# Attention with a gated MLP on one core: where block sums, half additions and value loads stand in the unit order

## The chip, the core and the metric

The kernel runs on one core of a Trainium2 chip. Its five engines have queues of their own: TensorE (PE in the profile, its weight loads PEld) multiplies matrices, VectorE (DVE) and ScalarE (ACT) work on elements, GpSimd (POOL) does here half of an addition and issues a few transfers, and SyncE (SP) issues nearly all DMA transfers. An engine runs its instructions in the order of the program and waits on semaphores for the others. The metric is the device time of one execution in microseconds (us), as the median of several runs. One further execution is profiled; all rows are from that one.

## The reference

```python
xn = _layernorm(x, axis=-1)                       # x: 1 x 2048 x 512
q = (xn @ wq).reshape(B, Sq, H, Dh)               # H = 32 heads, Dh = 128
scores = einsum("bhqd,bhkd->bhqk", q, k_cache) * Dh ** -0.5     # 2048 keys
o = einsum("bhqk,bhkd->bhqd", softmax(scores), v_cache)
s = o.reshape(B, Sq, H * Dh) @ wo                 # 4096 -> 512
h  = gelu(layernorm(xn) @ w1);  hs = shifted(h) @ w2;  x1 = xn + hs
h2 = gelu(layernorm(x1) @ w3) @ w4
out = x + s * silu(x1 + h2)
```

The attention over 32 heads is nearly all of the work. The MLP's gate is computed first and stored in DRAM until the output is put together. Everything is in bf16 with sums in f32.

## The kernel before, in words

The main loop runs over 128 units. A unit is one head with one block of 512 queries; the order is 8 groups of 4 heads, in each group the 4 query blocks, in each block the 4 heads. So unit 16g + 4qt + hh is head hh of group g with query block qt. A unit has 8 slots (SPU), and the loop from L1131 on goes over all slots n = 8u + p and writes out by hand, for slot p of unit u, what each engine gets next. Every instruction is pinned to that order, so an operation that is entered in another slot stands at another place of its engine's queue.

In a slot, TensorE multiplies two key chunks of 128 with the unit's queries into one of two PSUM tiles (`s_slot`, `ps_s`), ScalarE exponentiates it (L446, `pT<-ps_s`), and TensorE multiplies the values with the exponentials of ten slots ago (`pv_slot`, `ps_o<-pT,vb`).

The denominators of the softmax come from VectorE: `add_first` (L452) adds the first two `pT` tiles of a unit in slot 4, the third tile is added in slot 6, the fourth in slot 0 of the next unit, then `fold` and `fold_last` shrink the result to 128x512. The third tile is added in one of two ways. Outside the set `APART` it is one VectorE addition of 128x2048 (`add_next`, L461). Inside, GpSimd adds one half in slot 6 and VectorE the other half in slot 0 of the next unit (`add_half`, both L457).

From there the sums take a way through SP's queue. In slot 3 of the next unit the folded tile is transposed by a DMA (`turn`, L494, `tT<-acc`); in slot 0 of the unit after that VectorE sums it (`turned_sums`, L499) and takes reciprocals (L505), SP writes them to DRAM (L507, `dr<-rc`), in slot 1 SP reads them back on all partitions (`bcast`, L511, `rb<-dr`), and in slot 7 VectorE scales the unit's output with them (`norm`, L523). SP issues in order, and a transfer that waits for a semaphore holds all behind it.

The query projections of pairs of heads (units 14 to 125) and most of the output projections are done with seven products in place of eight, on sums and differences of blocks. VectorE makes these:

- `x_sum(qt, i)` (L366): sums of blocks of the normalised input, four for each query block, sixteen in all, entered by the list at L1120. One of them is written in place into `xnT`.
- `w_sum(h, i)` (L375): differences of query weights for the pair of heads h, h+1, entered at L1123. For head pair 2 all four stand in unit 11.
- `wo_sum(g, i)` (L562): differences of the output weights of a group, entered at L1084, four for each group.
- `o_sum` (L571): sums of the attention outputs of a block.

TensorE's products (`ps_q`, `ps_wo`) follow in fixed slots. The `ps_wo` tile has one buffer, so the next product into it waits until VectorE has added the last one to the accumulators (`wo_take`, L596). The queries of a pair are put together by ScalarE and VectorE (L415, L423 to L431), the last piece (L431) in slot 6 of the unit ahead of the pair.

Loads for the next group are spread over the loop from L993: b is the first unit of a group's last query block. Keys come in four transposing transfers for each head (`load_k`, L147), values in two halves of 256 KB (`load_v`, L159), issued in slot 6 of units b-2, b-1 (first head), b+2, b+3, b+4, b+5, b+6 and b+7 (fourth head). At the end of each slot the entries of `todo` run, so a value load of slot 6 stands in SP's queue behind the turned sums of slot 3 and the key load of slot 5, and ahead of the reciprocals of the next unit. The last head's value tile has a column of ones and is loaded in four pieces; `open_vx` opens it and sets that column.

The pool for block sums (`pS`) opens only when the MLP's held products are done, in unit 7.

Of the kernel before, what the change touches and what calls it, by code (L numbers as in the profile page):

```python
# [11 lines left out]
BF16 = mybir.dt.bfloat16  # L12
# [5 lines left out]
def kernel(  # L18
# [16 lines left out]
    P = nc.NUM_PARTITIONS  # L35
# [3 lines left out]
    Sq, D = x2d.shape  # L39
# [11 lines left out]
    HG = 4  # L51
    NG = H // HG

    SPU = KC // 2
# [34 lines left out]
    qtp = ent(pool("qt", 6))  # L89
# [11 lines left out]
    pR = right.enter_context(pool("pR", side="right", reuse_waits="tile"))  # L101
# [21 lines left out]
    HEAD = 7  # L123
# [11 lines left out]
    def at(n, fn):  # L135
        todo[n].append(fn)
# [194 lines left out]
               xnT[:, dc, qt * 512:(qt + 1) * 512], dc == 0, dc == DC - 1)  # L331

    def q_copy(u, eng=None):
        pl, tag = (pR, "qR") if u < HEAD else (qtp, "qT")
        qT = pl.tile([P, 512], BF16, tag=tag, **(dict(bufs=HEAD) if u < HEAD else {}), name="qT")
        src, dst = st[u].pop("psq")[:], qT[:]
        if u in TURN:
            src = src.rearrange("d (r j) -> d j r", j=4)
            dst = dst.rearrange("d (j r) -> d j r", j=4)
        if eng is None:  # L340
            pin(nc.vector.tensor_copy(out=dst, in_=src))
        else:
            pin(nc.scalar.activation(out=dst, in_=src, func=ACT.Identity))
        st[u]["qT"] = qT[:]
# [208 lines left out]
    def wo_sum(g, i):  # L553
        w = wog[g]
        b11, b12, b21, b22 = (w[:, k, c] for k in (UP, DOWN) for c in (WL, WR))
        if i == 2 and g < NG - 2:
            out = b12
        else:
            j = 0 if i == 2 else i
            out = pS.tile([P, 2, D // 2], BF16, tag=f"tw{j}", bufs=TW[j], name="tw")[:]  # L560
        a, b = ((b12, b11), (b22, tw.get((g, 0))), (b22, b12), (b21, tw.get((g, 1))))[i]
        pin(nc.vector.tensor_tensor(out=out, in0=a, in1=b, op=ALU.subtract))  # L562
        tw[g, i] = out
# [426 lines left out]
    pS = None  # L990
    for h in range(HG):
        load_wo(h)
    for g in range(NG - 1):  # L993
        b = (g * QT + QT - 1) * HG
        for hh in range(HG):
            h = (g + 1) * HG + hh
            for i, u in enumerate(((-10, -9, -8, -7), (-6, -5, -2, -1) if g else (-4, -3, -2, -1), (1, 1, 2, 3), (4, 5, 5, 6))[hh]):
                at((b + u) * SPU + 5, lambda h=h, i=i: load_k(h, (i,)))
            for i in range(2):
                at((b + (-2, 2, 4, 6)[hh] + i) * SPU + 6, lambda h=h, i=i: load_v(h, (i,)))  # L1000
            if h == H - 1:
                at((b + 6) * SPU + 3, open_vx)
            at((b + (-3, -3, 0, 0)[hh]) * SPU + (5, 7)[hh % 2], lambda h=h: load_w(h))
            at((b - 4 - hh // 2) * SPU + (5, 7)[hh % 2], lambda h=h: load_wo(h))

# [47 lines left out]

    FIRST, LAST = 14, NU - 4
    BLOCK = [(g, qt) for g in range(NG - 1) for qt in range(QT)][1:-2]
    APART = range(2 * HG + 1, NU - 3)
    pairs = range(FIRST, LAST + 1, 2)
    q_plan = defaultdict(list)
    steps = defaultdict(list)
# [21 lines left out]
            which[u0 + n].append((o_sum, g, qt, i))  # L1081
    for g in range(NG - 1):
        u0 = ((g * QT + (g == 0)) * HG + 6) * SPU
        for i, n in ((0, -4), (2, -4 if 0 < g < NG - 2 else 4), (1, 4), (3, 12)):  # L1084
            o_early[u0 + n].append((wo_sum, g, i))
    for i, (qt, u) in enumerate((qt, qt * HG + 5 + j) for qt in range(1, QT) for j in range(2)):
        at(u * SPU + 6, lambda qt=qt, i=i: sa_clear(qt, i % 2))
# [29 lines left out]
        for fn, *args in plan.get(n, ()):  # L1117
            fn(*args)

    for j, u in enumerate((9, 9, 9, 9, 12, 12, 13, 13, 13, 16, 17, 17, 18, 19, 20, 20)):  # L1120
        at(u * SPU + 3, lambda qt=(j // 4 - 1) % QT, i=j % 4: x_sum(qt, i))
    for h in range(2, H, 2):
        for i, u in enumerate((((-4, -3, -3, -3), (-1, -1, 0, 0))[h % HG // 2] if h >= HG else (11,) * 4)):  # L1123
            o_early[(h // HG * QT * HG + u) * SPU + 4].append((w_sum, h, i))

    for v in range(1, NU):
# [242 lines left out]
```

## Time and profile before

| | us |
|---|---|
| median of three runs | 1224.51 |
| lowest and highest run | 1224.1 and 1224.75 |
| the profiled execution, its time | 1222.83 |
| the same, its span from first to last instruction | 1221.1 |
| granted TensorE clock, mean | 1.000 |

The page gives for each engine its busy time with the share of the span and the count of instructions, then the chain that ended last, followed back from the end, as shares by engine. A row of a stretch gives the window in us from the start of the span, its length, the busy time of PE, PEld, DVE, ACT and POOL with the count of instructions, the granted clock, the share of the DMA engines and their GB/s. A row in order of time gives start and duration in us, engine, line, operation, out<-in, the shape, the count of equal instructions merged into the row, and in brackets the idle time of the engine just before it with what ended it. Instructions on one engine overlap a little, so what one costs is the step from its start to the next start, which is shorter than its duration. Some matmul records are missing (a row then says x1 where others say x2), and ends of matmuls are modelled, so for TensorE too starts are compared. "DMA to landing" is the time from the issue of a transfer to its completion.

### The profile page before, as it was taken

The page shows a single profiled execution, that of the slowest core. Times are in us where ns is not written, and L with a number is a line of the kernel's source. Part 1 is how long each engine was busy: PE and PEld are TensorE (multiplying, and loading weights), DVE is VectorE, ACT ScalarE, POOL GpSimd, SP SyncE. Part 2 cuts the span into 40 slices and gives each one's busy share as a digit, 9 for nine tenths or more (in the row PEclk, how much of TensorE's full clock was granted, in tenths as well). Part 3 has the DMA queues.
Part 4 walks back from the last instruction along what each step waited for, and adds up shares of the span by engine and source line. Part 5 has one row for each costly group of instructions (what it writes and reads, how often), then busy time and mean ns, then how long its engine had stood idle before and what let it go on. Part 6 is the DMA issues. An engine that isn't in the chain of part 4 may idle for free.

```text
span 1221.1 us, 18821 instructions
## 1 busy us (share of the span) xinstructions
PE 1208.6 (99%) x6534; PEld 673.7 (55%) x6657; DVE 1089.9 (89%) x1931; ACT 1107.6 (91%) x1243; POOL 297.6 (24%) x221
## 2 busy tenths in 40 slices
PE   9999999999999999999999999999999999999998
PEld 6466444555555555555555555555555555555555
DVE  7863778999999999999999899999999999989997
ACT  6345999999999999999999999999999999999996
POOL 5300001233222222222222222222222222223320
PEclk9999999999999999999999999999999999999999
DMA  7662323434343434344344433444433534455552
GB/s 178 169 153 59 56 57 83 96 85 98 75 90 88 99 66 90 85 99 88 70 95 84 103 69 83 92 96 78 87 83 91 100 66 90 87 101 110 124 113 66
DMA packets 248159, 113.07 MB, mean 93 GB/s; under 512 B 195328, under 2 KB 231296, under 8 KB 248064
## 3 DMA queue, kind: packets, MB, share of 16 engines
q1 hardware_dynamic: 244560, 107.21, 40.9%
q0 software_dynamic: 2944, 4.20, 1.5%
q8 instruction: 52, 0.85, 0.3%
q14 instruction: 43, 0.35, 0.2%
q10 hardware_dynamic: 560, 0.46, 0.1%
HBM read 69.60 MB, written 4.45 MB: 61 GB/s over the span
## 4 chain that ended last, share of the span: by engine, by line
PE 92%; DVE 5%; issue 1%; DMA 1%; ACT 1%; SPq 0%; DVEq 0%; POOL 0%; ACTq 0%
PE ps_s L112 39%; PE ps_o L112 35%; PE ps_q L112 8%; PE ps_wo L112 8%; PE ps_m L112 3%; DVE acc L461 1%; DVE acc L452 1%; DVE sacc L596 1%; ACT pT L446 1%; DMA kT<-in_A_k_cache_dram 0%; DVE acc L457 0%; DVE sm L499 0%; DMA tT<-acc 0%; DMA xin<-in_A_x_dram 0%; PE ps_oh L112 0%
## 5 line engine op out<-in xcount | busy, mean ns | idle before, releaser
L446 ACT ACTIVATE pT<-ps_s 128x1024 bf16<-128x1024 f32 x1016 | 1016.6, 1028 | 44.5 <-PE ps_s L112 13.0
L112 PE MATMUL ps_s<-qT,kT 128*128 128x512 bf16 (+1 forms) x2056 | 607.5, 377 | 0.8 <-ACT pT L446 0.4
L112 PE MATMUL ps_o<-pT,vb 128*128 128x512 bf16 x1884 | 568.3, 379 | 4.7
L457 POOL TENSOR_TENSOR acc<-acc,pT 128x1024 bf16<-128x1024 bf16 x116 | 246.8, 2128 | 727.4 <-DVE acc L452 395.6
L112 PEld LDWEIGHTS <-vb 128*128 128x128 bf16 x1984 | 194.0, 98 | 216.5
L112 PEld LDWEIGHTS <-kT 128*128 128x128 bf16 x2064 | 231.0, 113 | 72.4 <-DVE qT L431 1.4
L461 DVE TENSOR_TENSOR acc<-acc,pT 128x2048 bf16<-128x2048 bf16 x138 | 168.9, 1224 | 21.5 <-ACT pT L446 5.5
L452 DVE TENSOR_TENSOR acc<-pT 128x2048 bf16<-128x2048 bf16 x127 | 154.7, 1218 | 11.2 <-ACT pT L446 11.1
L596 DVE TENSOR_TENSOR sacc<-ps_wo,sacc 128x512 f32<-128x512 f32 x200 | 121.6, 608 | 3.4 <-PE ps_wo L112 2.4
L523 DVE TENSOR_TENSOR oT<-ps_o,rb 128x512 bf16<-128x512 f32 x127 | 86.5, 681 | 6.6 <-DMA rb<-dr 5.9
L465 DVE TENSOR_TENSOR acc<-acc 128x1024 bf16<-128x1024 bf16 x127 | 87.3, 687 | 2.4
L499 DVE TENSOR_REDUCE sm<-tT 128x4 f32<-128x512 bf16 x124 | 83.9, 676 | 6.0 <-DMA tT<-acc 5.4
L457 DVE TENSOR_TENSOR acc<-acc,pT 128x1024 bf16<-128x1024 bf16 x116 | 79.6, 686 | 0.0
L112 PEld LDWEIGHTS <-wc 128*128 128x128 bf16 x448 | 43.8, 98 | 52.9
L112 PE MATMUL ps_wo<-wo_h,oT 128*128 128x256 bf16 (+1 forms) x294 | 70.7, 307 | 0.5
L112 PEld LDWEIGHTS <-oT 128*128 128x128 bf16 x428 | 41.6, 98 | 45.6
L112 PEld LDWEIGHTS <-so 128*128 128x128 bf16 x400 | 39.1, 98 | 48.4 <-issue 1.7
L112 PEld LDWEIGHTS <-wq_h 128*128 128x128 bf16 x396 | 38.7, 98 | 46.0
L112 PE MATMUL ps_q<-xnT,wq_h 128*128 128x256 bf16 (+1 forms) x281 | 58.2, 294 | 0.2
L301 ACT ACTIVATE h2T<-ps_s 128x1024 bf16<-128x1024 f32 x28 | 28.7, 1023 | 31.6 <-PE ps_s L112 31.6
L469 DVE TENSOR_TENSOR acc<-acc 128x512 bf16<-128x512 bf16 x127 | 53.4, 420 | 2.4
L112 PEld LDWEIGHTS <-w_sb 128*128 128x128 bf16 x368 | 33.5, 98 | 29.2
(134 smaller groups left out, 924.4 us busy)
## 6 DMA issues: line engine op xcount, KB each, us to landing
rb<-dr SPq DMA_DIRECT2D x127, 256.0 KB, 3.8
vb<-in_A_v_cache_dram SPq DMA_DIRECT2D x62, 256.0 KB, 3.0
wq_h<-in_A_wq_dram SPq DMA_DIRECT2D x32, 128.0 KB, 2.5
wo_h<-in_A_wo_dram SPq DMA_DIRECT2D x32, 128.0 KB, 2.3
w_sb<-in_B_w_dram SPq DMA_DIRECT2D x8, 256.0 KB, 4.6
kT<-in_A_k_cache_dram SPq DMA_TRANSPOSE x128, 2.6
gate<-xall POOLq DMA_DIRECT2D x16, 128.0 KB, 2.3
sacc<-in_A_x_dram POOLq DMA_DIRECT2D x8, 256.0 KB, 4.6
```

What stands on the lines that cost most here:

```text
L112: pin(nc.tensor.matmul(out=out, lhsT=lhsT, rhs=rhs, start=start, stop=stop, **kw))
L301: pin(nc.scalar.activation(out=h2[c][:, f], in_=ps[:], func=ACT.Gelu_apprx_tanh))
L446: pin(nc.scalar.activation(out=s["pT"][-1][:, jj:jj + 2, :], in_=sps[:], func=ACT.Exp, scale=SCALE))
L452: pin(nc.vector.tensor_tensor(out=s["acc"][:], in0=s["pT"][0][:], in1=s["pT"][1][:], op=ALU.add))
L457: pin(eng.tensor_tensor(out=a[:, part, :], in0=a[:, part, :], in1=e[:, part, :], op=ALU.add))
L461: pin(nc.vector.tensor_tensor(out=a[:], in0=a[:], in1=st[u]["pT"][i][:], op=ALU.add))
L465: pin(nc.vector.tensor_tensor(out=a[:, 0:2, :], in0=a[:, 0:2, :], in1=a[:, 2:4, :], op=ALU.add))
L469: pin(nc.vector.tensor_tensor(out=a[:, 0, :], in0=a[:, 0, :], in1=a[:, 1, :], op=ALU.add))
L499: pin(nc.vector.tensor_reduce(out=sm[:], in_=s["tT"][:], axis=mybir.AxisListType.X, op=ALU.add))
L523: pin(nc.vector.tensor_tensor(out=to, in0=o, in1=rb, op=ALU.mult))
L596: pin(nc.vector.tensor_tensor(out=out, in0=ps, in1=out, op=ALU.add))
```

## The change

Four things move; the arithmetic stays the same. Block sums: the list of units for the sixteen `x_sum` goes from 9 to 20 to 8 to 20, and the four `w_sum` of head pair 2 go from unit 11 to units 8 and 9. Half additions: `APART` begins with unit 8 in place of 9. Value loads: slot 2 in place of slot 6 of the same units, which puts them behind the broadcast of slot 1 and ahead of the turned sums of slot 3; `open_vx` goes one unit earlier. Output weight differences: the third one of the last group that is done this way goes from slot 4 of unit 102 to slot 4 of unit 101, and its buffer comes from the pool of query tiles; the last unit's queries get a buffer with a tag of their own there, so the others have five in place of six.

```diff
     def q_copy(u, eng=None):
-        pl, tag = (pR, "qR") if u < HEAD else (qtp, "qT")
-        qT = pl.tile([P, 512], BF16, tag=tag, **(dict(bufs=HEAD) if u < HEAD else {}), name="qT")
+        pl, tag, n = (pR, "qR", HEAD) if u < HEAD else (qtp, "qT", 5) if u < NU - 1 else (qtp, "qL", 1)
+        qT = pl.tile([P, 512], BF16, tag=tag, bufs=n, name="qT")
...
         if i == 2 and g < NG - 2:
             out = b12
+        elif i == 2:
+            out = qtp.tile([P, 2, D // 2], BF16, tag="qT", bufs=5, name="tw")[:]
         else:
-            j = 0 if i == 2 else i
-            out = pS.tile([P, 2, D // 2], BF16, tag=f"tw{j}", bufs=TW[j], name="tw")[:]
+            out = pS.tile([P, 2, D // 2], BF16, tag=f"tw{i}", bufs=TW[i], name="tw")[:]
...
-                at((b + (-2, 2, 4, 6)[hh] + i) * SPU + 6, lambda h=h, i=i: load_v(h, (i,)))
+                at((b + (-2, 2, 4, 6)[hh] + i) * SPU + 2, lambda h=h, i=i: load_v(h, (i,)))
             if h == H - 1:
-                at((b + 6) * SPU + 3, open_vx)
+                at((b + 5) * SPU + 3, open_vx)
...
-    APART = range(2 * HG + 1, NU - 3)
+    APART = range(2 * HG, NU - 3)
...
-        for i, n in ((0, -4), (2, -4 if 0 < g < NG - 2 else 4), (1, 4), (3, 12)):
+        for i, n in ((0, -4), (2, -4 if g else 4), (1, 4), (3, 12)):
             o_early[u0 + n].append((wo_sum, g, i))
...
-    for j, u in enumerate((9, 9, 9, 9, 12, 12, 13, 13, 13, 16, 17, 17, 18, 19, 20, 20)):
+    for j, u in enumerate((8, 8, 9, 9, 9, 9, 9, 11, 11, 13, 17, 17, 18, 19, 20, 20)):
         at(u * SPU + 3, lambda qt=(j // 4 - 1) % QT, i=j % 4: x_sum(qt, i))
     for h in range(2, H, 2):
-        for i, u in enumerate((((-4, -3, -3, -3), (-1, -1, 0, 0))[h % HG // 2] if h >= HG else (11,) * 4)):
+        for i, u in enumerate((((-4, -3, -3, -3), (-1, -1, 0, 0))[h % HG // 2] if h >= HG else (8, 8, 9, 9))):
             o_early[(h // HG * QT * HG + u) * SPU + 4].append((w_sum, h, i))
```

## The prediction

> **What bounds the kernel now.** I began with the busy times and with the chain that ended last, then cut the loop into stretches.
>
> ```profile
> PE 1208.6 (99%) x6534; PEld 673.7 (55%) x6657; DVE 1089.9 (89%) x1931; ACT 1107.6 (91%) x1243; POOL 297.6 (24%) x221
> PE 92%; DVE 5%; issue 1%; DMA 1%; ACT 1%; SPq 0%; DVEq 0%; POOL 0%; ACTq 0%
> 311.03:361.64 50.61, 50.35 (x273) 28.36 (x277) 47.31 (x82) 49.03 (x55) 13.09 (x7) 1.00 0.39 79
> ```
>
> TensorE is busy for 99% of the span and holds 92% of the chain. The last row is a stretch of six units (22 to 27, 8.435 us each) at a granted clock of 1.00, with TensorE busy in 50.35 of 50.61 us, VectorE in 47.31. The matmuls set this pace, and the change removes no matmul, so a gain can only come out of places where TensorE waits. I therefore searched the order of time of TensorE for steps that are longer than the same step elsewhere (two 128x512 matmuls step by 0.43, two 128x256 ones by 0.22):
>
> ```profile
> 232.72 0.59 PE L112 MATMUL ps_o<-pT,vb 128*128 128x512 bf16 x2
> 233.78 0.38 PE L112 MATMUL ps_wo<-wo_h,so 128*128 128x256 bf16 x2 [0.47 <-DVE sacc L596]
> 242.43 0.38 PE L112 MATMUL ps_wo<-tw,oT 128*128 128x256 bf16 x2
> 243.25 0.62 PE L112 MATMUL ps_s<-qT,kT 128*128 128x512 bf16 x2 [0.44 <-ACT pT L446]
> 267.72 0.59 PE L112 MATMUL ps_o<-pT,vb 128*128 128x512 bf16 x2
> 268.43 0.38 PE L112 MATMUL ps_wo<-wo_h,so 128*128 128x256 bf16 x2
> 867.57 0.38 PE L112 MATMUL ps_wo<-tw,oT 128*128 128x256 bf16 x2
> 868.18 0.62 PE L112 MATMUL ps_s<-qT,kT 128*128 128x512 bf16 x2 [0.23 <-DVE qT L431]
> 993.87 0.59 PE L112 MATMUL ps_o<-pT,vb 128*128 128x512 bf16 x2
> 994.58 0.38 PE L112 MATMUL ps_wo<-wo_h,so 128*128 128x256 bf16 x2
> ```
>
> Five steps are too long: 1.06 for 0.43 (unit 12, 0.63 lost), 0.82 for 0.22 (end of unit 13, 0.60), 0.71 for 0.43 (unit 16, 0.28), 0.61 for 0.22 (end of unit 87, 0.39) and 0.71 for 0.43 (unit 102, 0.28). Together 2.18 us, and I found no sixth of that size in the loop. What is late each time is VectorE:
>
> ```profile
> 198.15 1.23 DVE L461 TENSOR_TENSOR acc<-acc,pT 128x2048 bf16<-128x2048 bf16 x1 [0.41 <-ACT pT L446]
> 207.75 0.69 DVE L341 CAST qT<-ps_q 128x512 bf16<-128x512 f32 x1 [1.14 <-PE ps_q L112]
> 210.36 0.66 DVE L457 TENSOR_TENSOR acc<-acc,pT 128x1024 bf16<-128x1024 bf16 x1
> 217.25 0.69 DVE L499 TENSOR_REDUCE sm<-tT 128x4 f32<-128x512 bf16 x1
> 222.58 0.28 DVE L375 TENSOR_TENSOR wc<-wq_h 128x256 bf16<-128x256 bf16 x1
> 223.51 1.22 DVE L452 TENSOR_TENSOR acc<-pT 128x2048 bf16<-128x2048 bf16 x1
> 230.92 0.42 DVE L366 TENSOR_TENSOR xs<-xnT 128x512 bf16<-128x512 bf16 x1
> 231.71 0.28 DVE L375 TENSOR_TENSOR wc<-wq_h 128x256 bf16<-128x256 bf16 x1
> 242.51 0.68 DVE L431 TENSOR_TENSOR qT<-ps_q,tq 128x512 bf16<-128x512 f32 x1
> 267.70 0.68 DVE L596 TENSOR_TENSOR sacc<-ps_wo,sacc 128x512 f32<-128x512 f32 x1
> 992.04 0.42 DVE L562 TENSOR_TENSOR tw<-wo_h 128x512 bf16<-128x512 bf16 x1
> 992.37 0.42 DVE L562 TENSOR_TENSOR tw<-wo_h,tw 128x512 bf16<-128x512 bf16 x1
> 993.84 0.68 DVE L596 TENSOR_TENSOR sacc<-ps_wo,sacc 128x512 f32<-128x512 f32 x1
> ```
>
> Read them against the steps above. The product at 268.43 starts as the addition of 267.70 ends (268.38), that at 994.58 as the one of 993.84 ends (994.52). The wait at 243.25 is booked on ScalarE, but the queries of unit 14 are finished by the combination at 242.51, which ends at 243.19, so I take that for its cause. From the cast at 207.75 into unit 15 VectorE's operations stand back to back: there it is the late engine. Ahead of that it has two holes, 0.41 before 198.15 and 1.14 before 207.75.
>
> **The change part by part.** I price an operation by the step to the next one. A 128x512 block sum costs 0.34 (992.04 to 992.37) and 0.79 as a dependent pair (230.92 to 231.71); four weight sums cost 0.93 (222.58 to 223.51), so two cost 0.47.
>
> Into unit 8 go two block sums and two weight sums: +0.79 +0.47. In exchange the full addition of 1.23 becomes the half of 0.66: -0.57. The hole of 0.41 takes its part, which leaves VectorE 0.28 late. Unit 9 gets one block sum (five for four) and two weight sums: +0.34 +0.47, so 1.09 late ahead of the cast, and the hole of 1.14 there swallows it. Its price in time is 0; without that hole it would be 1.09. In unit 11 four weight sums leave and two block sums come: -0.93 +0.79, VectorE 0.14 early. In unit 12 two block sums leave: -0.79, so 0.93 early against 0.63 lost. In unit 13 two of three leave (one rewrites a block of xnT, one is another sum): -0.68, so 1.61 early against 1.23 lost so far. In unit 16 the only one leaves: another 0.34. All three early stalls are covered, with 0.30 to 0.38 to spare at the first two: 0.63 + 0.60 + 0.28 = 1.51 us gained. Bounds for these three: 0 (VectorE is held by something else) and 1.51, since TensorE's own pace is below that.
>
> The half addition that goes to GpSimd:
>
> ```profile
> 206.75 2.12 POOL L457 TENSOR_TENSOR acc<-acc,pT 128x1024 bf16<-128x1024 bf16 x1 [10.93 <-DVE acc L452]
> ```
>
> In unit 9 it runs from 206.75 to 208.87, while VectorE casts, and VectorE's own half follows at 210.36. Unit 8 gets the same order, and nothing on GpSimd stands in front of it but a store. The Trainium skill, "SBUF — State Buffer", section "Who interferes with whom", speaks against this part: a VectorE instruction with two inputs in SBUF and a GpSimd one that reads SBUF exclude each other for a whole instruction. By that rule a collision would turn the -0.57 of unit 8 into as much as +1.55; the trace keeps the cast's 0.69 in that window, and a cast from PSUM has no second SBUF input, so I leave the -0.57.
>
> The weight difference of group 6 (its third) goes from unit 102 to unit 101 and to another buffer. That takes one 0.33 step from before 993.84 against 0.28 lost: -0.28, a margin of 0.05, bounds 0 and -0.28. Unit 101 then holds two differences like unit 21 of group 1, and the stretch behind that (311.03 on) shows no stall. The tile for the last unit's queries is only a rename of one of the six buffers, and the marker column of the last value tile is set one unit earlier: 0 each.
>
> The value loads change place on SP's queue, 54 in the loop and 4 pieces for the last head: they stood behind the key load at the end of a unit and ahead of the next reciprocals; now they stand behind the broadcast and ahead of the turned sums (tT) and the key load.
>
> ```profile
> 210.47 0.34 SPq L507 DMA_DIRECT2D dr<-rc  x1
> 213.19 0.34 SPq L511 DMA_DIRECT2D rb<-dr  x1
> 213.59 1.20 SPq L494 DMA_TRANSPOSE tT<-acc  x1
> DMA to landing us min/median/max: 3.6/3.6/3.6
> 396.23 0.32 SPq L507 DMA_DIRECT2D dr<-rc  x1
> 398.59 0.32 SPq L511 DMA_DIRECT2D rb<-dr  x1
> 400.15 1.22 SPq L494 DMA_TRANSPOSE tT<-acc  x1
> DMA to landing us min/median/max: 2.5/2.5/2.5
> 403.12 0.68 DVE L499 TENSOR_REDUCE sm<-tT 128x4 f32<-128x512 bf16 x1
> vb<-in_A_v_cache_dram SPq DMA_DIRECT2D x62, 256.0 KB, 3.0
> dr<-rc SPq DMA_DIRECT2D x127, 2.0 KB, 1.7
> ```
>
> The two landing rows belong to the turned sums above them (units 10 and 32). Sent 0.40 behind the broadcast's 256 KB they land after 3.6, sent 1.56 behind it after 2.5: the broadcast's queue is gone some 1.6 us after its issue. A value load is 256 KB too, so I take 3.2 us for both. The broadcast itself comes earlier: the reciprocals took 2.36 there (396.23 to 398.59) with a value load in front, and the median is 1.7. With 0.7 less, the turned sums go out 2.3 behind the broadcast and land 0.9 us later than now. In unit 32 that is 403.5 instead of 402.65, and VectorE wants them at 403.12: a wait of 0.4. Per unit it idles (50.61 - 47.31) / 6 = 0.55, so I price it at 0. The bounds are no delay, and a start only once the values have landed: 0.35 + 3.0 + 1.2 behind the broadcast, then 2.5, which is 7.05 instead of 4.06, so 3.0 later. The value nearest to rows is the 0.9. The Trainium skill, "DMA: Bandwidth & Descriptors", section "Anatomy of one DMA — SWDGE (gpsimd) path", gives a fixed 2.0 us and bytes / 436e9, an estimate of 0.60 us for such a load on another kind of queue; by that the delay would be nil and this part 0 as well, and the 1.1 us more at 0.40 distance disagree with so short a stay.
>
> What a late landing of the turned sums does has two rows:
>
> ```profile
> 742.20 0.69 DVE L499 TENSOR_REDUCE sm<-tT 128x4 f32<-128x512 bf16 x1 [1.83 <-DMA tT<-acc]
> 860.11 0.69 DVE L499 TENSOR_REDUCE sm<-tT 128x4 f32<-128x512 bf16 x1 [0.70 <-DMA tT<-acc]
> ```
>
> The wait of 1.83 in unit 73 made no step of TensorE longer; that of 0.70 in unit 87 is followed by the 0.39 at 868.18, because three differences of a new group had filled VectorE just before. I take this fourth stall for chance: it may go, and another may come elsewhere, so 0 net, with -0.39 and +0.39 as bounds. Queued behind a value load that waits for its buffer are the turned sums, which have to wait for VectorE's last fold anyway.
>
> Sum: -1.51 - 0.28 + 0 = -1.79 us. The profiled execution took 1222.83 (span 1221.1 and 1.73 around it) and would take 1221.04. The median of the runs shown, 1224.51, is 1.68 above the profiled one; on it the sum gives 1222.72, and I say 1222.7.
>
> **Rivals.**
> *Units 10 to 13 stay late.* In unit 10 the reciprocals took 2.72 (210.47 to 213.19), so broadcast and turned sums went out together. If they are late again, the value load of unit 10 now goes between them and takes SP some 0.6: the turned sums are issued at about 214.2 with 512 KB in front. By the 3.2 above they land 3.2 - 1.0 = 2.2 later than the plain 2.5, at 218.9, and VectorE wants them at 217.25: 1.6 late, which uses up the 0.93 and the 1.61. Only the 0.28 of unit 102 and part of unit 16 are gained: about 1224.1. For it: the 2.72 is in the row. Against: most reciprocals take 1.7.
>
> *Value loads in front of the turned sums cost more than they spare.* This is the slower side, one mechanism in eight of every sixteen units. If the delay is not 0.9 but 2.0, VectorE waits 2.0 less the room of some 0.5 to 1.0, say 1.3 in 8 units, 10.4 us per group of 16, against an idle share of 16 x 0.55 = 8.8. The 1.6 over come back as waits of TensorE in nearly seven groups: +11, so 1224.5 - 1.8 + 11 = 1233.7. It decides from a delay of 1.9 on (8 x 1.1 = 8.8); a little below it, chance stalls of 0.4 as in unit 87 in about ten places would give 1226.7. For it: the 1.1 more behind a single broadcast. Against: the reciprocals come earlier by 0.7, and a single wait of 1.83 was absorbed whole.
>
> *More is gained than the profile holds.* The runs without a profile are 1.68 longer. If half of that is waits behind late DMAs of the kind of unit 87 and they go with the value loads' old place, the time is 1222.7 - 0.4 - 0.8 = 1221.5. For it: 2.36 against 1.7 for the reciprocals. Against: the 1.68 may be fixed time that no row shows.
>
> **How the numbers follow.** Two tenths of a per cent are 2.45 us, about what a measurement of this kernel can tell from no change: below 1222.06 is faster, above 1226.96 slower. My forecast (three early stalls and that of unit 102 gone) gets 0.58, the late units 0.18, the larger gain 0.15, the slower case 0.09. The first two count as no change (0.76), though the forecast lies below the lowest run shown; the third is faster (0.15), the fourth slower (0.09). The range starts at the larger gain with a little room, 1221.3, and ends past the late units, at 1225.0, where all of the 1.79 is lost and one or two stalls of 0.39 come: outside lie the slower case and a small rest.
>
> **What would show it.** The steps at units 12, 13, 16 and 102 are 0.43 and 0.22 again, and VectorE's hole before the cast of unit 9 is gone or nearly so. The turned sums land 3 to 3.6 us after their issue in units with a value load, the reciprocals in 1.4 to 1.7, and VectorE's waits for either stay under a microsecond each. I am wrong if the product of unit 12 still waits for the addition in front of it, if waits on the turned sums show up in most units with value loads, or if TensorE's steps are regular and the time is still above 1224.

## The result, and the profile after

The changed kernel takes 1230.27 us (median of 6 runs, 1227.02 to 1231.12) against 1224.49 us for the kernel before (6 runs, 1222.9 to 1225.2): a ratio of 1.0043, with a 95% interval of 1.0033 to 1.0053. It is slower by 5.8 us. The forecast was 1222.7, its range ended at 1225.0, and the slower side had been given a chance of 0.09. The profiled execution took 1230.29 us (span 1228.5), at a granted clock of 1.000 as before. The profiled execution of before, 1222.83, lies 1.7 below its median here, so the two traces differ by 7.5 us and the medians by 5.8.

Page of the kernel after: busy times, chain by engine, the two groups of VectorE that wait for SP's transfers, and one row of the DMA issues (count, size, median us from issue to landing):

```profile
PE 1218.6 (99%) x6657; PEld 672.8 (55%) x6657; DVE 1089.8 (89%) x1931; ACT 1108.6 (90%) x1243; POOL 299.1 (24%) x222
...
PE 77%; DVE 14%; DMA 6%; ACT 2%; issue 1%; DVEq 0%; POOL 0%; ACTq 0%
...
L499 DVE TENSOR_REDUCE sm<-tT 128x4 f32<-128x512 bf16 x124 | 84.3, 680 | 23.9 <-DMA tT<-acc 23.6
L523 DVE TENSOR_TENSOR oT<-ps_o,rb 128x512 bf16<-128x512 f32 x127 | 86.6, 682 | 6.9 <-DMA rb<-dr 6.3
...
vb<-in_A_v_cache_dram SPq DMA_DIRECT2D x62, 256.0 KB, 4.4
```

The same rows of the kernel before:

```profile
L523 DVE TENSOR_TENSOR oT<-ps_o,rb 128x512 bf16<-128x512 f32 x127 | 86.5, 681 | 6.6 <-DMA rb<-dr 5.9
...
L499 DVE TENSOR_REDUCE sm<-tT 128x4 f32<-128x512 bf16 x124 | 83.9, 676 | 6.0 <-DMA tT<-acc 5.4
```

VectorE does the same amount of work (1089.8 us busy, 1089.9 before), but it idles 23.9 us ahead of the turned sums (L499) where it idled 6.0; ahead of the use of the broadcast (L523) nothing changed. The value loads themselves take 4.4 from issue to landing where they took 3.0. In the chain of what ended last, TensorE's share falls from 92% to 77%, and VectorE and the DMAs take 14% and 6%. The PE counts differ because some matmul records were missing before; busy PE is not compared.

How much of that reaches TensorE can be worked out from the trace. I take the time from one unit's first score product to the next one's and subtract what the unit's products need at the loop's regular pace; what is left is the unit's lost time. Over units 9 to 123 it is 2.4 us before and 9.8 after. The difference, 7.4, is the whole difference of the two spans (1221.1 and 1228.5). By stretch, before and after: units 9 to 19 1.7 and 2.5; units 20 to 110 0.75 and 6.0; units 111 to 123 0 and 1.35. So 17.9 us more of waiting on VectorE became 7.4 us on TensorE, and most of it lies in the middle of the loop, where nothing was moved but the value loads and one weight difference (unit 101).

The loss is not spread evenly over the units with a value load ahead. In units 9 to 123, 19 units use turned sums that took 3.9 us or more from issue to landing, up to 6.41, and lose 7.3 of the 9.8. The 42 units whose sums landed behind a value load after 2.8 to 3.9 us, around the median of 3.37, lose 1.6 together. Before the change 11 units had sums of 3.9 or more, and lost 1.0.

**The longest wait in the middle of the loop, followed to its end.** SP in order of time, kernel after, units 50 and 51 (start, duration, issued transfer):

```profile
553.66 0.32 SPq L511 DMA_DIRECT2D rb<-dr  x1
554.03 0.43 SPq L159 DMA_DIRECT2D vb<-in_A_v_cache_dram  x1
555.75 1.21 SPq L494 DMA_TRANSPOSE tT<-acc  x1
...
563.60 0.32 SPq L511 DMA_DIRECT2D rb<-dr  x1
563.97 0.43 SPq L159 DMA_DIRECT2D vb<-in_A_v_cache_dram  x1
566.32 1.21 SPq L494 DMA_TRANSPOSE tT<-acc  x1
```

The landing of the transfer issued at 555.75, from the view of the tile tT in that stretch:

```profile
DMA to landing us min/median/max: 5.5/5.5/5.5
```

So it lands at 561.25, and VectorE, in order of time of the same kernel, has been waiting for it:

```profile
558.39 0.69 DVE L523 TENSOR_TENSOR oT<-ps_o,rb 128x512 bf16<-128x512 f32 x1
561.28 0.69 DVE L499 TENSOR_REDUCE sm<-tT 128x4 f32<-128x512 bf16 x1 [2.20 <-DMA tT<-acc]
562.00 0.18 DVE L505 RECIPROCAL rc<-sm 128x4 f32<-128x4 f32 x1
562.09 0.39 DVE L597 TENSOR_TENSOR sacc<-ps_wo,sacc 128x256 f32<-128x256 f32 x1
...
564.81 0.42 DVE L428 TENSOR_TENSOR qT<-ps_q,tq 128x256 bf16<-128x256 f32 x1
...
568.28 0.68 DVE L431 TENSOR_TENSOR qT<-ps_q,tq 128x512 bf16<-128x512 f32 x1
```

TensorE in order of time, same unit:

```profile
561.63 0.59 PE L112 MATMUL ps_o<-pT,vb 128*128 128x512 bf16 x2
562.54 0.38 PE L112 MATMUL ps_wo<-wo_h,oT 128*128 128x256 bf16 x2 [0.31 <-DVE sacc L597]
...
564.27 0.59 PE L112 MATMUL ps_o<-pT,vb 128*128 128x512 bf16 x2
565.29 0.38 PE L112 MATMUL ps_q<-xnT,wc 128*128 128x256 bf16 x2 [0.43 <-DVE qT L428]
...
568.53 0.38 PE L112 MATMUL ps_wo<-tw,oT 128*128 128x256 bf16 x2
569.02 0.62 PE L112 MATMUL ps_s<-qT,kT 128*128 128x512 bf16 x2
```

Read three steps: 562.54 - 561.63 = 0.91 for 0.43, 565.29 - 564.27 = 1.02 for 0.43, and 569.02 - 568.53 = 0.49 for 0.22. That is 0.48 + 0.59 + 0.27 = 1.34 us lost in one unit, behind one wait of 2.20. Each of the three products waits for a VectorE operation that stood behind the late sum: the addition L597 (ends 562.48), the queries L428 (end 565.23), the combination L431 (ends 568.96). The landing of 5.5 is far above the median of 3.37; why this one took so long stays open.

**Units 10 to 12.** SP in order of time, unit 10, kernel after:

```profile
210.79 0.34 SPq L507 DMA_DIRECT2D dr<-rc  x1
213.51 0.34 SPq L511 DMA_DIRECT2D rb<-dr  x1
213.90 0.43 SPq L159 DMA_DIRECT2D vb<-in_A_v_cache_dram  x1
214.42 1.20 SPq L494 DMA_TRANSPOSE tT<-acc  x1
```

VectorE in order of time, from the hole of unit 9 to unit 11:

```profile
201.28 0.66 DVE L457 TENSOR_TENSOR acc<-acc,pT 128x1024 bf16<-128x1024 bf16 x1
...
208.08 0.68 DVE L341 CAST qT<-ps_q 128x512 bf16<-128x512 f32 x1
...
217.39 0.69 DVE L523 TENSOR_TENSOR oT<-ps_o,rb 128x512 bf16<-128x512 f32 x1 [0.43 <-DMA rb<-dr]
218.70 0.69 DVE L499 TENSOR_REDUCE sm<-tT 128x4 f32<-128x512 bf16 x1 [0.62 <-DMA tT<-acc]
```

TensorE in order of time, unit 12:

```profile
233.36 0.59 PE L112 MATMUL ps_o<-pT,vb 128*128 128x512 bf16 x2
234.45 0.38 PE L112 MATMUL ps_wo<-wo_h,so 128*128 128x256 bf16 x2 [0.50 <-DVE sacc L597]
```

The cast of unit 9 starts at 208.08 without a hole in front (it was 207.75 behind a hole of 1.14): the three more block sums, the four weight sums and the half addition (0.66, not lengthened) that units 8 and 9 got went in at a third of a microsecond. Then the reciprocals of unit 10 take 2.72 again (210.79 to 213.51), the value load stands between the broadcast and the turned sums, VectorE waits 0.43 and 0.62, and the product of unit 12 steps by 1.09 for 0.43. With two smaller ones ahead of it the unit loses 1.11. In units 13, 16 and 102 the long steps of before are gone.

### The profile page after: what moved, and what is told of

Read it like the earlier page. It is cut to its first block, busy times and chain, and to the rows that moved or that the text cites. A ratio compares the mean times of both kernels' runs of the same rounds, so it can differ in the third digit from the quotient of the medians.

```text
span 1228.5 us, 18899 instructions
## 1 busy us (share of the span) xinstructions
PE 1218.6 (99%) x6657; PEld 672.8 (55%) x6657; DVE 1089.8 (89%) x1931; ACT 1108.6 (90%) x1243; POOL 299.1 (24%) x222
## 4 chain that ended last, share of the span: by engine, by line
PE 77%; DVE 14%; DMA 6%; ACT 2%; issue 1%; DVEq 0%; POOL 0%; ACTq 0%
PE ps_s L112 32%; PE ps_o L112 29%; PE ps_q L112 6%; PE ps_wo L112 6%; DMA tT<-acc 4%; PE ps_m L112 3%; DVE acc L461 3%; DVE acc L452 1%; DVE sacc L597 1%; DVE sm L499 1%; ACT pT L446 1%; DVE acc L457 1%; DVE acc L469 1%; DVE acc L465 1%; DMA rb<-dr 1%
## 5 line engine op out<-in xcount | busy, mean ns | idle before, releaser
L112 PE MATMUL ps_o<-pT,vb 128*128 128x512 bf16 x1984 | 589.9, 379 | 0.0
L461 DVE TENSOR_TENSOR acc<-acc,pT 128x2048 bf16<-128x2048 bf16 x137 | 167.7, 1224 | 21.6 <-ACT pT L446 5.1
L452 DVE TENSOR_TENSOR acc<-pT 128x2048 bf16<-128x2048 bf16 x127 | 154.8, 1219 | 10.7 <-ACT pT L446 10.5
L597 DVE TENSOR_TENSOR sacc<-ps_wo,sacc 128x512 f32<-128x512 f32 x200 | 121.5, 607 | 1.4 <-PE ps_wo L112 0.8
L499 DVE TENSOR_REDUCE sm<-tT 128x4 f32<-128x512 bf16 x124 | 84.3, 680 | 23.9 <-DMA tT<-acc 23.6
L523 DVE TENSOR_TENSOR oT<-ps_o,rb 128x512 bf16<-128x512 f32 x127 | 86.6, 682 | 6.9 <-DMA rb<-dr 6.3
L469 DVE TENSOR_TENSOR acc<-acc 128x512 bf16<-128x512 bf16 x127 | 53.4, 421 | 2.4
```

The lines of the kernel that those rows point to most:

```text
L112: pin(nc.tensor.matmul(out=out, lhsT=lhsT, rhs=rhs, start=start, stop=stop, **kw))
L452: pin(nc.vector.tensor_tensor(out=s["acc"][:], in0=s["pT"][0][:], in1=s["pT"][1][:], op=ALU.add))
L461: pin(nc.vector.tensor_tensor(out=a[:], in0=a[:], in1=st[u]["pT"][i][:], op=ALU.add))
L469: pin(nc.vector.tensor_tensor(out=a[:, 0, :], in0=a[:, 0, :], in1=a[:, 1, :], op=ALU.add))
L499: pin(nc.vector.tensor_reduce(out=sm[:], in_=s["tT"][:], axis=mybir.AxisListType.X, op=ALU.add))
L523: pin(nc.vector.tensor_tensor(out=to, in0=o, in1=rb, op=ALU.mult))
```

## The experiments

All ratios are to the kernel before in runs on the same chip. Its median was 1227.0 on the chip of the sums alone, the value loads alone, the place behind the turned sums and half the bytes; 1224.9 on the chip of the repeat, the old sums, the place ahead of the broadcast and double the bytes; 1225.0 on that same chip for the first group and the lighter VectorE; and 1225.8 for the two other queues. So the ratios are compared, not the times. Ratios from different sets of runs still differ: the change itself gave 1.0043 at first and 1.0070 in the repeat, so a difference of 0.3% between two sets needs no cause in the kernel. "Loaded units" are the 43 units of 20 to 110 in which a value load is issued behind the broadcast, and lost time is worked out as above.

### The parts one at a time

Sums alone, the changed kernel with the value loads back in slot 6:

```diff
-                at((b + (-2, 2, 4, 6)[hh] + i) * SPU + 2, lambda h=h, i=i: load_v(h, (i,)))
+                at((b + (-2, 2, 4, 6)[hh] + i) * SPU + 6, lambda h=h, i=i: load_v(h, (i,)))
```

> The changed kernel with the value loads back in slot 6; block sums, half additions and the output weight difference stay where the change put them. Theory (the value loads ahead of the turned sums cost the time): VectorE's idle time on the turned sums (L499) falls from 23.9 us back to about 6, the long steps of TensorE at units 12, 13, 16 and 102 are gone, time about 1222.7, between 1221.5 and 1224. Rival (the moved sums overload VectorE in units 8 to 12 and that lag is carried on): the time stays above 1228 and the waits remain.

Measured: 1224.44, ratio 0.9986 (0.9978 to 0.9995). VectorE's idle time ahead of the turned sums, from its page:

```profile
L499 DVE TENSOR_REDUCE sm<-tT 128x4 f32<-128x512 bf16 x124 | 83.9, 677 | 6.1 <-DMA tT<-acc 5.8
```

The moved sums gain 0.14%, 1.7 us, and leave that idle time where it was (6.0). Units 12, 13, 16 and 102 lose nothing in its trace. The time in microseconds lies above the 1224 that I had set; the kernel before takes 1227.0 on this chip.

Value loads alone, the kernel before with the loads (and the marker column of the last value tile) moved:

```diff
-                at((b + (-2, 2, 4, 6)[hh] + i) * SPU + 6, lambda h=h, i=i: load_v(h, (i,)))
+                at((b + (-2, 2, 4, 6)[hh] + i) * SPU + 2, lambda h=h, i=i: load_v(h, (i,)))
...
-                at((b + 6) * SPU + 3, open_vx)
+                at((b + 5) * SPU + 3, open_vx)
```

> The kernel before with the value loads (and the opening of the last value tile) moved as in the change, nothing else. Theory: about 1224.5 + 7 = 1231.5 (1229 to 1234), VectorE idle on the turned sums 20 us or more. Rival (the moved sums): 1224.5, idle about 6.

Measured: 1236.97, ratio 1.0087 (1.0074 to 1.0100). Its page:

```profile
L499 DVE TENSOR_REDUCE sm<-tT 128x4 f32<-128x512 bf16 x124 | 84.2, 679 | 28.1 <-DMA tT<-acc 27.5
```

That is beyond my 1229 to 1234 and, as a ratio, more than the change as a whole: the whole loss comes from the value loads. The steps of units 13 (0.60) and 102 (0.27) stand as in the kernel before, and unit 12 loses 1.9.

A repeat of the changed kernel gives the spread of these figures from one set of runs to another:

> The changed kernel once more, unaltered, on the same chip as these others. Theory: ratio 1.003 to 1.006 again, idle time on the turned sums above 20 us, steps lengthened in other units than in its first profile where those hung on single late landings, and in the same units (11, 12, 15, 48, 51) where they hang on the place of the value loads.

Measured: ratio 1.0070 (1.0056 to 1.0084); VectorE idled 27.8 us ahead of the turned sums, and TensorE lost 13.5. The ratio is above the 1.006 that I had set; units 11, 12, 15, 48 and 51 lose 0.1 to 1.35 again. Of the loss, 11.0 lies in the 26 units whose sums took 3.9 us or more. The cost of the loads is thus 0.6 to 0.9% (1.0043 or 1.0070 over 0.9986, or 1.0087 directly).

### The place on the queue

Behind the turned sums in place of ahead of them, everything else as changed:

```diff
-                at((b + (-2, 2, 4, 6)[hh] + i) * SPU + 2, lambda h=h, i=i: load_v(h, (i,)))
+                at((b + (-2, 2, 4, 6)[hh] + i) * SPU + 3, lambda h=h, i=i: load_v(h, (i,)))
```

> The changed kernel with the value loads in slot 3, directly behind the turned sums' transfer and ahead of the key load. Theory (only what stands in front of the turned sums counts): the turned sums land 2.4 to 2.6 us after issue in most units, the reciprocals in 1.4, time 1222.7 or less (1221.5 to 1223.5). Rival (any earlier value load disturbs, by sharing the queues with the broadcast or the key load): the time stays at 1227 or above.

Measured: 1222.86, ratio 0.9968 (0.9958 to 0.9978): faster than both kernels. Chain and group from its page:

```profile
PE 86%; DVE 8%; DMA 4%; ACT 1%; issue 1%; SPq 0%; DVEq 0%; ACTq 0%
...
L499 DVE TENSOR_REDUCE sm<-tT 128x4 f32<-128x512 bf16 x124 | 83.8, 676 | 4.3 <-DMA tT<-acc 4.0
```

One slot later, the load goes out some 1.26 us after the turned sums, and these land after 2.5 us again (median of the loaded units). The reciprocals' store takes 1.64 there (I had set 1.4), against 2.09 with the loads in slot 6 of the kernel before and 2.21 in slot 6 of the changed kernel. With the moved sums slot 3 is thus 1.6 us faster than slot 6 (1222.86 against 1224.44, on one chip). That the shorter store is the reason is not shown.

The same place in the kernel before, with its old block sums (and `open_vx` one unit earlier):

> The kernel before with the value loads in slot 3, behind the turned sums; block sums, half additions and weight difference as before. Theory (the two parts of the change are independent, the sums give 0.14%): 0.1 to 0.2% above the version with both, so a ratio of 0.998 to 0.999, with the long steps at units 12, 13, 16 and 102 of the kernel before. Rival (the gain of 0.3% came from the place behind the turned sums alone): ratio 0.997.

Measured: 0.9997 (0.9988 to 1.0006). Units 12, 13, 15, 16 and 102 lose 0.90, 0.61, 0.59, 0.49 and 0.28. Both forecasts missed: the ratio lies just above 0.999 and far from 0.997. The place alone gains nothing that can be measured, the sums alone 0.14%, the two together 0.32%. The first of these comes from another chip than the other two, so whether the parts add up is not shown.

Ahead of the broadcast, between the reciprocals' store and the broadcast:

```diff
+    vpre = defaultdict(list)
...
-                at((b + (-2, 2, 4, 6)[hh] + i) * SPU + 2, lambda h=h, i=i: load_v(h, (i,)))
+                vpre[(b + (-2, 2, 4, 6)[hh] + i) * SPU + 1].append(lambda h=h, i=i: load_v(h, (i,)))
...
+        for fn in vpre.pop(n, ()):
+            fn()
```

> The changed kernel with the value loads ahead of the broadcast, while SP waits for the reciprocals to land: issued some 1.4 us earlier than in the change. Theory (drain of 512 KB in some 3.2 us from the first issue): the turned sums land after 2.5 to 2.9 us, the broadcast later by up to 1.3; VectorE's idle time on L499 falls below 12 us, that on L523 rises above 10; ratio 0.998 to 1.004. Rival (two transfers ahead of the turned sums cost the same wherever they stand): turned sums 3.3 us or more, ratio 1.004 or above.

Measured: ratio 1.0004 (0.9995 to 1.0013). The turned sums land after 2.9 at the median of the loaded units, VectorE idles 4.4 ahead of them and 13.2 ahead of L523. That second figure was 6.6 before, 6.9 with the change and 11.7 and 10.2 in the two kernels whose loads stand in slot 6 and in slot 3, so whether some of the wait has moved to the broadcast stays open; the broadcast does go out later, 2.28 after the reciprocals' store at the median where the change has 1.47. The ratio is 1.0004, so no gain of the sums is left to be seen here.

### The dose

Half the bytes ahead (pieces of 128 KB, one in slot 2, one in slot 6):

```diff
-    def load_v(h, halves):
+    def load_v(h, halves, n=2):
...
-            w = KSPLIT // 2
+            w = KSPLIT // n
...
-                at((b + (-2, 2, 4, 6)[hh] + i) * SPU + 2, lambda h=h, i=i: load_v(h, (i,)))
+                for k in range(2):
+                    at((b + (-2, 2, 4, 6)[hh] + i) * SPU + (2, 6)[k], lambda h=h, j=2 * i + k: load_v(h, (j,), 4))
```

> The changed kernel with each 256 KB value load cut in two pieces of 128 KB, one in slot 2 ahead of the turned sums and one in slot 6. Theory of a queue that drains at a fixed rate: half the bytes ahead delay the turned sums by some 0.3 to 0.5 us instead of 1, most of which VectorE's slack takes: 1223 to 1226, idle on L499 10 us or less. Rival (each transfer ahead costs its own fixed time, whatever its size): as slow as the changed kernel, 1229 to 1232.

Measured: 1226.61, ratio 1.0000 (0.9991 to 1.0009). The idle time is just above the 10 that I had set, and the time above 1226, on the chip where the kernel before takes 1227.0.

```profile
L499 DVE TENSOR_REDUCE sm<-tT 128x4 f32<-128x512 bf16 x124 | 84.0, 678 | 10.7 <-DMA tT<-acc 10.6
```

Double the bytes ahead in half the units (both halves of a head in slot 2 of the first unit):

```diff
-                at((b + (-2, 2, 4, 6)[hh] + i) * SPU + 2, lambda h=h, i=i: load_v(h, (i,)))
+                at((b + (-2, 2, 4, 6)[hh]) * SPU + 2, lambda h=h, i=i: load_v(h, (i,)))
```

> The changed kernel with both halves of a head's values (512 KB) in slot 2 of the first of its two units, none in the second: the same bytes in all, twice as many ahead of half as many turned sums. So far 0, 128 and 256 KB ahead gave medians of about 2.5, 2.84 and 3.37 us for the turned sums. Theory (a queue that drains at a fixed rate, and VectorE's slack runs out): about 4.5 to 4.9 us in the 27 units concerned, waits on the turned sums of 1 to 2 us each there, slower than the changed kernel: ratio to the kernel before 1.006 to 1.015. Rival (a fixed price for each unit that has a value load ahead): half as many such units, about half the loss, ratio 1.002.

Measured: 1251.27, ratio 1.0211 (1.0196 to 1.0227), beyond what I had expected.

```profile
L499 DVE TENSOR_REDUCE sm<-tT 128x4 f32<-128x512 bf16 x124 | 84.2, 679 | 46.7 <-DMA tT<-acc 46.7
```

TensorE loses 37.3 us in units 9 to 123, 7.3 of it in unit 115 alone, where VectorE waited 4.68. This trace is of the slowest of the five executions (1258.39), and not all of its loss is waiting. TensorE in order of time, the two waits, and the two stretches in which its granted clock was 0.50 (the clock stands third from the end):

```profile
573.43 0.38 PE L112 MATMUL ps_wo<-wo_h,oT 128*128 128x256 bf16 x2 [2.00 <-DVE sacc L597]
1135.11 0.58 PE L112 MATMUL ps_q<-xnT,wc 128*128 128x256 bf16 x2 [4.27 <-DVE qT L428]
...
574.40:577.80 3.40, 3.40 (x12) 1.52 (x10) 3.33 (x7) 1.92 (x2) 0.00 (x0) 0.50 0.30 57
1134.20:1141.00 6.80, 5.89 (x16) 2.31 (x16) 5.28 (x10) 2.20 (x3) 3.00 (x2) 0.50 0.30 77
```

By half of the busy 3.40 and 5.89 us, an estimate, the lower clock costs some 4.6 of the 37.3 us. The traces of before and of the change have no such stretch inside the loop. The four figures stand together (delay: median time from issue to landing of the turned sums in the loaded units, less the 2.49 of the kernel before; the ratio over that of the sums alone, 0.9986):

| KB ahead of the turned sums | issue to landing, us | delay, us | idle ahead of L499, us | ratio / 0.9986 |
|---|---|---|---|---|
| 0 (sums alone) | 2.58 | 0.1 | 6.1 | 1 |
| 128 | 2.85 | 0.36 | 10.7 | 1.0014 |
| 256 (the change; its repeat) | 3.37; 3.38 | 0.88; 0.89 | 23.9; 27.8 | 1.0057; 1.0084 |
| 512, in half as many units | 4.44 | 1.95 | 46.7 | 1.0225 |

The rows of 0 and 128 KB are of one chip, the repeat and the row of 512 KB of another, and the last idle time is of the slowest execution. The delay grows roughly evenly with the bytes, some 0.9 us for each 256 KB. The cost grows faster than the delay. That fits a room on VectorE that is used up first, but at 512 KB a part is the halved clock.

### The first group

The changed kernel with the loads of the first group alone (units 10 to 19) back in slot 6:

```diff
-                at((b + (-2, 2, 4, 6)[hh] + i) * SPU + 2, lambda h=h, i=i: load_v(h, (i,)))
+                at((b + (-2, 2, 4, 6)[hh] + i) * SPU + (2 if g else 6), lambda h=h, i=i: load_v(h, (i,)))
```

> The changed kernel with the value loads of units 10 to 19 (for group 1) back in slot 6, all others in slot 2. Theory (the three early steps were removed by the moved sums and came back only because the value loads of units 10 and 11 held the turned sums): TensorE's steps at units 11, 12, 13 and 17 are regular or nearly so (1.0 us or less lost in units 9 to 19, against 2.5 and 2.9 in the two profiles of the change), the later ones as in the change; ratio about 0.2% below the change, 1.002 to 1.005. Rival (the moved sums themselves make units 11 and 12 late): 2 us or more lost in units 9 to 19, ratio unchanged at 1.004 to 1.007.

Measured: ratio 1.0037 (1.0025 to 1.0048). Units 9 to 19 lose 1.26 against 2.48 and 2.87 in the two traces of the change; units 11, 12, 13 and 17 are regular, and 1.08 stays in unit 15, so the 1.0 that I had set was just missed. By the traces the early units are worth 1.2 to 1.6 us. The ratio falls by 0.06% from the change's first measurement and by 0.33% from its repeat on this chip, so their share is not settled; most of the loss over the sums alone (0.9986) stays.

### More room on VectorE

The changed kernel without the last fold (L469) in units 8 to 123, so that the denominators there take in half of the keys only:

```diff
+        if u in TURN and u >= 2 * HG:
+            return
```

> The changed kernel without VectorE's last fold of the sums (L470, a 128x512 addition of 0.34 us a unit) in units 8 to 123. The sums then cover half of the keys. Theory (the 0.9 us of delay only costs because VectorE has too little room behind the turned sums): with 0.34 us less work in each unit and the turned sums sent 0.34 earlier, the waits on L499 fall from 24 to 10 us or less and TensorE loses 3 us or less in units 9 to 123; ratio 0.997 to 1.001. Rival (the value loads disturb TensorE through something else than VectorE, such as late values or keys): ratio 1.004 or above.

Measured: 1225.28, ratio 1.0000 (0.9990 to 1.0009). Busy times and the sums' group from its page:

```profile
PE 1209.3 (99%) x6534; PEld 672.9 (55%) x6657; DVE 1051.2 (86%) x1815; ACT 1107.5 (91%) x1243; POOL 299.4 (24%) x222
...
L501 DVE TENSOR_REDUCE sm<-tT 128x4 f32<-128x512 bf16 x124 | 84.4, 680 | 29.7 <-DMA tT<-acc 29.5
```

One part missed: I expected the waits to shrink, and they came to 29.7, against 23.9 and 27.8 in the two traces of the change. At the median of the loaded units the turned sums go out 0.57 earlier in the unit than in the change but land only 0.37 earlier, 3.8 after issue. The other part came in the ratio, and in direction on TensorE: with 38.6 us less work in 116 units, 0.33 a unit, it loses 4.4 us in units 9 to 123 in place of 9.8 and 13.5, though I had set 3. About as much waiting costs half as much or less once VectorE has a third of a microsecond more of room in each unit. The kernel before without its last fold was not run, so how much of the 2.4 us that it loses anyway would go too is not known. For the rival of late values or keys there is no sign: TensorE's waits that the two traces of the change book end with VectorE or ScalarE, none with a transfer.

### Another engine's queue

Is it the place in SP's line that counts, or the traffic? The loads were issued in the same slot by ScalarE, and then by GpSimd:

```diff
-                pin(nc.sync.dma_start(out=dst[:, ks], in_=v[:, ks]))
+                pin((nc.scalar if h >= HG else nc.sync).dma_start(out=dst[:, ks], in_=v[:, ks]))
```

> The changed kernel with its value loads issued by ScalarE in place of SP, in the same slot 2. Theory (the turned sums stand in line behind the values on SP's own queue): with the values on another queue the turned sums of the loaded units land in 2.4 to 2.7 us after their issue at the median, as in the units without a load, and VectorE idles 4 to 10 us on them; ScalarE pays some 0.4 us for each issue. Rival (the 16 DMA engines are shared, whoever issues): the landing stays at 3.1 to 3.5 us and the idle time of VectorE on them above 18 us. The ratio to before is 0.996 to 1.002 by the theory unless ScalarE's issues stall the exponentials, and 1.003 or more by the rival.

Measured: ratio 1.0032 (1.0021 to 1.0043). My theory fell: in the loaded units the turned sums land after 3.46, though no value load stands in SP's line any more. VectorE idles less ahead of them, 15.4 (between the two forecasts), and more ahead of L523, 13.7. SP, and then ScalarE, in order of time in unit 51 of this kernel:

```profile
561.05 0.32 SPq L511 DMA_DIRECT2D rb<-dr  x1
563.77 1.22 SPq L494 DMA_TRANSPOSE tT<-acc  x1
```

```profile
560.11 0.38 ACTq L159 DMA_DIRECT2D vb<-in_A_v_cache_dram  x1
```

The load goes out 0.94 ahead of the broadcast here, and 0.28 ahead of it at the median of the loaded units. At that median it stands 2.2 us ahead of the turned sums, where SP's load of the change stands 2.05 ahead.

> The changed kernel with its value loads issued by GpSimd in place of SP, in the same slot of the written order; GpSimd does little else, so a load may go out earlier than the broadcast. Theory (standing in line on SP's queue is what makes the turned sums late): landing 2.4 to 2.7 us in the loaded units at the median, VectorE idles 4 to 10 us on them, ratio 0.996 to 1.000. Rival (shared engines): landing above 3 us or late reciprocals in their place (above 2 us at the median), ratio 1.000 to 1.006.

Here the line reads `nc.gpsimd` in place of `nc.scalar`. Measured: ratio 1.0061 (1.0041 to 1.0082). GpSimd sends the load as soon as its half addition is done, so in unit 50 it goes out together with the reciprocals' store, which SP issues at 551.64. GpSimd in order of time:

```profile
549.57 2.12 POOL L457 TENSOR_TENSOR acc<-acc,pT 128x1024 bf16<-128x1024 bf16 x1 [5.06 <-ACT pT L446]
551.63 0.72 POOL L159 DMA_DIRECT2D vb<-in_A_v_cache_dram  x1
```

The reciprocals take 2.19 at the median of the loaded units, the turned sums 3.47, and VectorE idles 20.3 ahead of L523 and 11.1 ahead of L499. So the traffic delays the small transfers also when it does not stand in SP's line. How long a load delays them is not the same for each place and queue: GpSimd's goes out 3.9 us ahead of the turned sums at the median, and SP's ahead of the broadcast stands 3.7 ahead of them with a landing of 2.9. The Trainium skill has the rule behind it in "DMA: Bandwidth & Descriptors", section "Issuing engines are not separate DMA queues": transfers started by any engine run on the same 16 DMA engines and interleave. Both traces agree that another issuer does not spare the turned sums (3.46 and 3.47 where 2.5 is the undisturbed landing).

## Why the prediction was wrong

**Right: the moved sums.** The hole of unit 9 took them, the half additions ran at their usual length, and the third difference of group 6 left unit 102 regular (unit 101 loses 0.15). Forecast -1.79 us, measured by the sums alone 0.14%, 1.7 us. That these agree to a tenth is luck: the interval of 0.9978 to 0.9995 stands for 0.6 to 2.7 us, and the trace of the sums alone, regular at the four units, loses 4.1 us at others (15, 21, 23, 37, 51, 87 and 119) where that of before lost 2.4 in all. The collision that the Trainium skill describes ("SBUF — State Buffer", section "Who interferes with whom") does not show in the units that the change touched: VectorE's half at 201.28 takes 0.66, and what VectorE does while GpSimd's runs (198.41 to 200.53 in unit 8) reads PSUM or has one input. Elsewhere it does show. VectorE and GpSimd in order of time, kernel after:

```profile
1140.36 0.90 DVE L457 TENSOR_TENSOR acc<-acc,pT 128x1024 bf16<-128x1024 bf16 x1
```

```profile
1138.59 2.12 POOL L457 TENSOR_TENSOR acc<-acc,pT 128x1024 bf16<-128x1024 bf16 x1 [6.31 <-DVE acc L452]
```

VectorE's half starts 0.34 before GpSimd's ends (1140.71) and takes 0.90 in place of 0.66 to 0.68. Five of the 117 halves after overlap by 0.31 to 0.34 and take 0.86 to 0.90; before, three do. So the forecast was right to leave it out of unit 8, and as it is as rare before, it does not explain the loss.

**Right in size: the delay of the turned sums.** "the turned sums go out 2.3 behind the broadcast and land 0.9 us later than now": 0.88 was measured in the loaded units. The estimate by the Trainium skill's rule ("DMA: Bandwidth & Descriptors", section "Anatomy of one DMA — SWDGE (gpsimd) path"), 0.60 us for 256 KB, from which I had taken a delay of nil, does not hold here: the delay is 0.88. The picture behind the 0.9 was only half right: I let SP's queue drain one transfer after the other, and a load on ScalarE's queue at nearly the same time delays the turned sums just as much (3.46). And the 0.9 holds for the median alone: the landings behind a value load run from 2.65 to 6.41.

**Wrong: the price of the delay.** The step that failed is "Per unit it idles (50.61 - 47.31) / 6 = 0.55, so I price it at 0". It takes one delay, 0.9, for all 54 loads and one room, 0.55, for all units. Neither was so. Around the median delay the price is indeed near nothing (1.6 us in 42 units), but 19 units used sums that landed after 3.9 us or more, and they hold 7.3 of the 9.8 us lost. And the 0.55 is an average: in units of the kernel before that wait for nothing, VectorE idles only 0.20 to 0.37; the rest lies in other units, or behind the operation that TensorE needs. In unit 51 a wait of 2.20 came out as 1.34 in three steps. The kernel without the last fold is the test of the room: 0.33 a unit more of it, waits no smaller, and the loss on TensorE down from 9.8 to 4.4, nearly all of which (4.2) again lies in units with sums of 3.9 us or more. Why some landings took so long is not shown.

With the price that the runs showed the sum would be: 1.7 gained by the sums and 7.0 to 10.3 lost by the loads (0.0057 to 0.0084 of 1224.5, from the table), 5 to 9 slower.

**The slower rival was the right mechanism with the wrong threshold.** It was to decide "from a delay of 1.9 on (8 x 1.1 = 8.8)", from the same average. On the chip a delay of 0.36 uses up the sums' gain, 0.88 costs 0.6 to 0.8%, and 1.95, in half of the units, about 2%. Its side line, "chance stalls of 0.4 as in unit 87 in about ten places would give 1226.7", came nearest to the kind of loss: 17 units between 11 and 123 lose 0.12 to 1.33 each in the trace of the change.

**The rival of units 10 to 13 came true as well.** The reciprocals of unit 10 took 2.72 again and unit 12 lost 1.11. With the loads of the first group put back it loses nothing; by the traces that is 1.2 us, in a difference of 7.4.

**Open.** The evidence for 0 was unit 73, where a wait of 1.83 was absorbed whole, against unit 87, which I took for chance. Which of the two a unit resembles depends on what its VectorE has to do before TensorE's next need; I have followed that through in units 12 and 51 only. The lost time of single profiled executions also varies for the same kernel (9.8 and 13.5), so single units are not to be compared to a tenth.

## What to carry to other kernels

The mean idle time of an engine says little about how long a wait it can take, and a median delay says little about what the long ones cost: look for the operation behind the wait that the bounding engine needs next, and for the time by which that operation was early before. When a bulk load is moved, look which small, urgent transfer is issued in the microseconds after it, on any queue; with the load right behind that transfer the ratio was 0.9968, with the load ahead of it 1.0043 and 1.0070 (in other sets of runs). A part of a change that gains (here the moved sums) is worth measuring apart from the part that does not.

## What the runs showed of the hardware that I had not expected

- 128, 256 and 512 KB sent ahead of a transposing transfer of a 128x512 bf16 tile delay its landing by 0.36, 0.88 and 1.95 us at the median, 260 to 360 KB for each microsecond. Another issuer does not help: 3.37 from SP, 3.46 from ScalarE at nearly the same time, 3.47 from GpSimd, whose loads went out earlier.
- While TensorE waited 4.27 us in the kernel with 512 KB ahead, its granted clock went to 0.50 and stayed there for 6.8 us; behind a wait of 2.00 it was 0.50 for 3.4 us.
- A VectorE addition of two 128x1024 tiles that started 0.34 us before GpSimd's addition of the other half ended took 0.90 us in place of 0.66 to 0.68; GpSimd's kept its 2.12.
- A store of 2 KB of reciprocals takes 1.4 us in units without a load and 2.1 to 2.2 with a value load in flight (slot 6, and GpSimd's). In unit 10 SP's broadcast follows it 2.72 us later in both kernels (210.79 to 213.51 after), and no run explains that place.
- The kernel before itself ran at 1224.5 to 1227.0 (medians on different chips), 0.2% apart: more than the gain of the sums.
